# Spreading feed-forward parts over the half-steps of a unit of attention: a share for the half-step of the first product with V

## The chip, the cores and the metric

One of the eight cores of a Trainium2 chip runs the program. Times are device microseconds (us) of one execution, taken as the median of several runs; one further execution was recorded by the hardware profiler, and every row of a profile is from that one. The engines are TensorE (PE; its weight loads are PEld), VectorE (DVE), ScalarE (ACT), GpSimd (POOL) and SyncE (SP), which issues the DMAs.

## The reference

```python
x = A_x                                   # [1, 2048, 512]
mod = (silu(c) @ w_mod).reshape(1, 6, 1, 512)
sa, ca, ga, sb, cb, gb = mod's six rows
h = layernorm(x) * (1 + ca) + sa
q = (h @ wq) as 32 heads of 16            # k = h @ wk, v = h @ wv: one head of 16
p = softmax(q k^T / 4)                    # 2048 x 2048 for each head
x = x + ga * ((p @ v, heads side by side) @ wo)
h = layernorm(x) * (1 + cb) + sb
x = x + gb * ((sigmoid(h @ w_gate) * (h @ w_up)) @ w_down)     # F = 1792
```

Everything is float32. The kernel forms most products from numbers split into a high and a low half of 16 bits, in three passes (high x high, high x low, low x high).

## The kernel before

A first stage (`PLAN`, some 110 us) loads the input, makes k, V and the first queries, and begins the maxima. Then comes the main stage, which the change touches, and behind it a tail with what is left of the feed-forward layer for the last 512 rows.

**The main stage** runs over 32 units: 8 blocks of 256 queries by 4 groups of 8 heads. A unit has 16 steps of 128 keys, a step `s` has two half-steps `h`, so there are 1024 half-steps. In each of them the program emits for TensorE, in the order `ORDER = "a0", "s0", "c", "a1", "s1"`:

- `a0` and `a1`: scores whose maxima VectorE takes (`a_tile`, PSUM tiles `sa`, three banks, reduced into `mx`). They run more than a unit ahead.
- `s0` and `s1`: scores once more, transposed (`st_tile`, PSUM tiles `st`, two banks), of which ScalarE takes the exponential into `P`.
- `c`: the product of `P` with V (`pv`, PSUM tensor `craw`), two steps (`LAG`) behind the scores, in float32, followed by a hand-over: a matmul with a block of zeros (`nought`) on whose end the next product waits.
- a *piece*: so many *parts* of whatever else TensorE has to do (`piece`).

All of these are 64 x 32 tiles. The `a` and `s` of a half-step lie on one half of the rows, the product with V on the other, and in the next half-step the halves are exchanged. The order on TensorE, VectorE and ScalarE is that of the program (`keep`).

**A unit's end.** `craw` is one bank. After the last product of a unit (step `t = NKB - 1`, `h = 1`) ScalarE copies it out (`unit_end`, tile `cs`), and the first product of the next unit (`t = 0`, `h = 0`) waits for that copy. The exponentials behind it in ScalarE's queue come after it.

**Parts.** The other work comes in couples of two groups of matmuls that accumulate in two banks (`Couple`): one part is 8 matmuls of 64 x 32 tiles with 512 columns, four on either half of the rows. There are query couples (24 parts, tiles `pq`, before `FIRST = 140` steps are over), couples with wo (24, `po`), with gate and up (24, `pgu`) and with down (48 or 36, `pd`). `plan` takes the next couple when the one before is used up and asks `places` how many parts each half-step gets: the couple's two halves are laid out over as many half-steps as their weights times a rate come to (`RATE = 2.2` parts, `QRATE = 0.55` for query couples), and rounded cumulatively. `weight` gives the weight of one half-step. Before the change it is:

- 0 for the half-step of a unit's first product with V,
- `SWAP / RATE`, that is 5 parts, for that of the last product (1 for query couples),
- for the others what makes the sum of a unit 32 (1 for query couples, whose sum is 31).

`lead` carries what a couple is ahead or behind on to the next. For query couples the first three half-steps of a couple get nothing (`skip`).

Of the kernel before, what the change touches and what calls it, by code (L numbers as in the profile page):

```python
# [26 lines left out]
NKB = S // P  # L27
# [38 lines left out]
RATE = 2.2  # L66
# [2 lines left out]
AHEAD = 0, 0, 0, 0  # L69
MOST = 3  # L70
SWAP = 5
WSTEPS = 110
WLAST = 175
WLATE = 2
# [14 lines left out]
def adaln_mqa_glu_kernel(  # L89
# [928 lines left out]

    def weight(hb, q):
        s, h = divmod(hb, 2)
        t = (s - LAG) % NKB
        if s >= LAG and (t, h) == (0, 0):
            return 0.0
        if (t, h) == (NKB - 1, 1):
            return SWAP / RATE if not q else 1.0
        return 1.0 if q else (2 - SWAP / RATE + 2 * (NKB - 1)) / (2 * NKB - 2)

    def places(m, hb, rate, most, skip, part):  # L1030
        ws = []
        rate, most = rate / part, most / part
        while sum(ws) * rate < m + lead[0] / part - rate / 2 or sum(ws) * most < m:
            ws.append(0.0 if len(ws) < (skip or 0) else weight(hb + len(ws), skip is not None))
        lead[0] += part * (m - rate * sum(ws))
        ends = [round(m * sum(ws[:k + 1]) / sum(ws)) for k in range(len(ws))]
        return [k - z for z, k in zip([0] + ends, ends)]
# [28 lines left out]
    def plan(s, hb):  # L1066
        if run:
            return
        g = pick(s)
        if g is None:  # L1070
            lead[0] = 0.0
            return
        if g.stage == "tr":
            sizes = [4]
        else:
            q = g.stage == "q" and s < FIRST
            light = not q and g.stage == "gu" and s < 2 * NU * NKB + SKIP
            rate, most = (QRATE, 1) if q else (ERATE, 2) if light else (RATE, MOST)
            sizes = []
            for leg in range(2):  # L1080
                sizes += places(g.n // 2, hb + len(sizes), rate, most, (3 if leg == 0 else 0) if q else 0 if light else None, g.w)
            if hb + len(sizes) > 2 * len(units) * NKB:
                spare.insert(0, g)
                return
        at = 0
        for z in sizes:
            run.append((g, at, at + z))
            at += z
        assert at == g.n, (at, g.n, g.stage)
# [12 lines left out]
    for i, (b, o) in enumerate(units):  # L1102
# [11 lines left out]
        for kb in range(NKB):  # L1114
# [30 lines left out]
            while wdone < nw:  # L1145
                if wdone < nw - 4 and (wdone + 0.5) * WSTEPS > (s + 1) * (nw - 4):
                    break
# [68 lines left out]
```

## Time and profile before

| | |
|---|---|
| median of 3 runs | 1707.13 us (1706.41 to 1707.3) |
| the profiled execution's own time | 1703.12 us |
| its span, first to last instruction | 1701.3 us |
| busy: PE, PEld, DVE, ACT, POOL | 1657.1, 997.2, 1427.7, 1287.3, 610.2 us |
| mean granted TensorE clock | 0.993 |

A row of a group of instructions gives: line, engine, operation, output <- inputs, shapes, count | busy time in us, mean ns of one | idle time of the engine before them, with what ended it. A row of a timeline gives: start in us, length in us, engine, line, operation, names, count, and in brackets idle time ahead of it. A row of windows gives: the stretch, its length, then busy time and count of each engine, the granted clock, the DMA engines' busy share and GB/s. Most instructions go through one helper and so bear line 135; they are told apart by their tiles. Ends of matmuls are modelled, so the starts are the better measure.

### The profile page before, as it was taken

What the parts mean: (1) busy time and instruction counts of PE and PEld (TensorE: products, weight loads), DVE (VectorE), ACT (ScalarE), POOL (GpSimd) and SP (SyncE); (2) the same over time, 40 slices, a digit from 0 to 9 for tenths busy, and PEclk for the clock granted to TensorE, in tenths of its full rate; (3) what the DMA queues carried; (4) which work ended last, traced back from release to release, by engine and by line L of the source; (5) the groups of instructions that cost most, each with busy time, mean ns of one, the idle gap of its engine ahead of it and who ended that gap; (6) DMA issues with size and microseconds to landing.
All of it is one profiled execution on the core that took longest, in us unless ns stands there. A gap on an engine that the chain in (4) does not pass through costs nothing.

```text
span 1701.3 us, 88793 instructions
## 1 busy us (share of the span) xinstructions
PE 1657.1 (97%) x40226; PEld 997.2 (59%) x40226; DVE 1427.7 (84%) x2428; ACT 1287.3 (76%) x2335; POOL 610.2 (36%) x784
## 2 busy tenths in 40 slices
PE   6999999999999999999999999999999999999998
PEld 3335555555456666666656676666666676654443
DVE  7799999989999999999999999999999999912311
ACT  5558898878988888888888888888888888884100
POOL 4432554553242451232443232223442332132423
PEclk9989999999999999999999999999999999999999
DMA  7121333320121110111021110010121110011211
GB/s 243 54 62 49 107 104 99 110 77 21 29 62 50 58 54 14 40 28 28 28 77 52 50 42 13 28 37 25 38 77 41 52 53 16 23 47 52 87 50 38
DMA packets 86726, 94.12 MB, mean 55 GB/s; under 512 B 24916, under 2 KB 65868, under 8 KB 86348
## 3 DMA queue, kind: packets, MB, share of 16 engines
q1 hardware_dynamic: 86348, 88.44, 16.8%
q8 instruction: 315, 5.16, 1.3%
q14 instruction: 63, 0.52, 0.1%
HBM read 67.82 MB, written 16.24 MB: 49 GB/s over the span
## 4 chain that ended last, share of the span: by engine, by line
PE 81%; DVE 11%; ACT 3%; SPq 2%; DMA 2%; issue 1%; POOL 1%; POOLq 0%; ACTq 0%; DVEq 0%
PE craw L135 21%; PE pgu L135 15%; PE sa L135 13%; PE st L135 12%; DVE mx L135 8%; PE pd L135 7%; PE pgu L186 5%; PE pd L186 3%; PE po L135 2%; PE pq L135 2%; SPq L135 1%; ACT P L135 1%; DVE st L135 1%; DMA xall<-in_A_x_dram 1%; DMA lc<-lD 1%
## 5 line engine op out<-in xcount | busy, mean ns | idle before, releaser
L135 DVE TENSOR_REDUCE mx<-sa 128x1 f32<-128x512 f32 x2048 | 1288.6, 682 | 82.3 <-PE st L135 40.5
L135 ACT ACTIVATE P<-st 128x512 f32<-128x512 f32 x2048 | 1167.4, 597 | 226.2 <-PE st L135 168.6
L135 PE MATMUL craw<-P,V 64*32 64x512 f32 x8192 | 1094.7, 599 | 1.3 <-ACT cs L135 0.5
L135 PE MATMUL sa<-kp,qp 64*32 64x512 f16 (+1 forms) x7940 | 834.7, 379 | 13.1 <-DVE mx L135 12.4
L135 PE MATMUL st<-qp,kp 64*32 64x512 f16 x8192 | 837.6, 379 | 4.9 <-ACT P L135 4.2
L135 PEld LDWEIGHTS <-kp 64*32 64x32 f16 x8192 | 333.9, 91 | 215.9 <-issue 93.4
L135 PEld LDWEIGHTS <-qp 64*32 64x32 f16 (+1 forms) x7940 | 288.4, 92 | 149.6 <-issue 74.2
L135 PE MATMUL pgu<-h2h,gw 64*32 64x512 f16 x5248 | 285.4, 376 | 0.6
L135 PEld LDWEIGHTS <-gw 64*32 64x32 f16 x7872 | 181.7, 92 | 66.8 <-issue 25.1
L135 PEld LDWEIGHTS craw<-P,V 64*32 64x32 f32 x8192 | 184.0, 105 | 23.7 <-PE craw L135 4.1
L135 PE MATMUL pgu<-h2l,gw 64*32 64x512 f16 x2624 | 178.8, 376 | 1.2 <-issue 1.0
L135 PE MATMUL craw<-nought 64*32 64x1 f16 x1050 | 171.2, 163 | 0.0
L897 POOL TENSOR_SCALAR th<-th 128x512 f32<-128x512 f32 x41 | 25.4, 620 | 355.0 <-ACT th L135 298.2
L135 PEld LDWEIGHTS <-nought 64*32 64x32 f16 x1050 | 97.7, 93 | 71.9 <-issue 51.5
L556 POOL MEMSET qp<- 32x1024 f16 x60 | 56.7, 945 | 79.3 <-PE st L135 57.2
L320 POOL TENSOR_SCALAR wst<-wst 128x512 f32<-128x512 f32 x46 | 28.6, 621 | 155.5 <-DMA wst<-in_B_w_up_dram 103.2
L135 PE MATMUL pd<-wdl,gh 64*32 64x512 f16 x1152 | 79.2, 376 | 0.0
L135 PE MATMUL pd<-wdh,gh 64*32 64x512 f16 x1152 | 77.3, 376 | 0.1
L135 PE MATMUL pd<-wdh,gl 64*32 64x512 f16 x1152 | 76.6, 376 | 0.0
L186 PE MATMUL pgu<-h2h,gw 128*128 128x512 f16 x240 | 71.9, 379 | 1.5 <-DVE h2h L355 1.5
L891 ACT ACTIVATE th<-pgu 128x512 f32<-128x512 f32 x15 | 9.0, 597 | 82.1 <-PE pgu L186 82.1
L135 DVE COPY u<-pgu 128x512 f32<-128x512 f32 x41 | 28.0, 682 | 50.1 <-PE pgu L135 50.1
(160 smaller groups left out, 1436.9 us busy)
## 6 DMA issues: line engine op xcount, KB each, us to landing
gw<-wD SPq DMA_DIRECT2D x56, 512.0 KB
wD<-gw SPq DMA_DIRECT2D x14, 512.0 KB
wm<-in_w_mod_dram SPq DMA_DIRECT2D x6, 1024.0 KB
qp<-qD SPq DMA_DIRECT2D x192, 32.0 KB
qD<-q SPq DMA_DIRECT2D x16, 256.0 KB
xr<-in_A_x_dram SPq DMA_DIRECT2D x16, 256.0 KB
out_dram<-ot SPq DMA_DIRECT2D x16, 256.0 KB
raw<-cs SPq DMA_DIRECT2D x248, 16.0 KB
```

Source lines behind the costliest of these rows:

```text
L135: return (lambda *a, **k: keep(f_(*a, **k))) if pinned else f_
L186: pe.matmul(cut[0](self.bank) if cut else self.bank, l_, r_, start=(n == 0), stop=(n == self.n - 1))
L320: pool.tensor_scalar(w_, w_, SW, 0.0, op0=ALU.mult, op1=ALU.add)
L556: eng.memset(qp[j:j + 32], 0.0)
L891: act.activation(th, p_, AF.Tanh, scale=0.5 / (SH * SW))
L897: pool.tensor_scalar(th, th, 1.0, 1.0, op0=ALU.add, op1=ALU.mult)
```

## The change

Three things change in `weight` and what calls it: the half-step of a unit's first product with V gets the weight `FRESH = 0.9` instead of 0; the weight of the last half-step is 5 parts at whatever rate the couple has, so also for query couples; and the other half-steps' weight makes the sum of a unit 32 in both kinds. The rate is passed in, before it is divided by a group's width.

```diff
+FRESH = 0.9
...
-    def weight(hb, q):
+    def weight(hb, rate):
         s, h = divmod(hb, 2)
         t = (s - LAG) % NKB
         if s >= LAG and (t, h) == (0, 0):
-            return 0.0
+            return FRESH
         if (t, h) == (NKB - 1, 1):
-            return SWAP / RATE if not q else 1.0
-        return 1.0 if q else (2 - SWAP / RATE + 2 * (NKB - 1)) / (2 * NKB - 2)
+            return SWAP / rate
+        return (2 * NKB - FRESH - SWAP / rate) / (2 * NKB - 2)

     def places(m, hb, rate, most, skip, part):
-        ws = []
+        ws, full = [], rate
         rate, most = rate / part, most / part
         while sum(ws) * rate < m + lead[0] / part - rate / 2 or sum(ws) * most < m:
-            ws.append(0.0 if len(ws) < (skip or 0) else weight(hb + len(ws), skip is not None))
+            ws.append(0.0 if len(ws) < (skip or 0) else weight(hb + len(ws), full))
```

## The prediction

> **What bounds the kernel now.** I read the page first, then the windows of single units, then the timeline of unit boundaries.
>
> ```profile
> L135 DVE TENSOR_REDUCE mx<-sa 128x1 f32<-128x512 f32 x2048 | 1288.6, 682 | 82.3 <-PE st L135 40.5
> L135 ACT ACTIVATE P<-st 128x512 f32<-128x512 f32 x2048 | 1167.4, 597 | 226.2 <-PE st L135 168.6
> ```
>
> Both groups run 2048 times, twice in each of the 1024 half-steps of attention. Back to back a maximum costs VectorE 0.63 us (1288.6/2048) and an exponential costs ScalarE 0.57 us, so a half-step takes VectorE about 1.26 us whatever TensorE does. One more operation recurs, once per unit: the eviction cs of the bank that collects P times V.
>
> ```profile
> L135 ACT ACTIVATE cs<-craw x32: 590/597/603, 151.0 to 1559.3; 128x512 f32<-128x512 f32 x32
> ```
>
> From the first to the last of these lie 31 units: (1559.3 - 151.0)/31 = 45.4 us a unit. Two kinds of unit are to be told apart. The windows (length, then busy time and count of PE, PEld, DVE, ACT, POOL; granted clock) of one stretch with query couples and two units with feed-forward parts:
>
> ```profile
> 192.60:234.30 41.70, 40.36 (x934) 21.03 (x927) 39.82 (x70) 37.34 (x70) 19.51 (x26) 1.00 0.31 93
> ...
> 909.20:955.10 45.90, 45.90 (x1378) 30.85 (x1372) 43.20 (x72) 38.49 (x71) 14.73 (x17) 1.00 0.16 49
> 955.10:1001.00 45.90, 45.87 (x1380) 31.91 (x1366) 42.78 (x71) 38.55 (x71) 14.74 (x17) 1.00 0.16 49
> ```
>
> In the query unit VectorE is busy 39.82 of 41.70 us (95%): it sets the pace. In the feed-forward units it is busy 94%, and TensorE 100% by records whose ends are modelled. Which one paces can't be read off these shares; it is read off what one part more costs. Here are stretches of 28 half-steps (from the product with V of a unit's fourth half-step to that of its last), shortest load first; the count of matmuls grows by 8 for each part:
>
> ```profile
> 1335.53:1374.96 39.43, 39.40 (x1194) 1.00 0.18 55
> ...
> 1426.99:1466.49 39.50, 39.44 (x1205) 1.00 0.06 16
> ...
> 913.89:953.74 39.85, 39.85 (x1210) 1.00 0.18 55
> 1097.09:1137.14 40.05, 40.05 (x1214) 1.00 0.14 41
> 543.12:583.28 40.16, 40.15 (x1222) 1.00 0.21 61
> 1288.67:1329.23 40.56, 40.36 (x1222) 1.00 0.18 54
> ```
>
> 28 matmuls more (3.5 parts) go with (40.16 + 40.56)/2 - 39.43 = 0.93 us more: 0.27 us a part. So in the middle of a feed-forward unit TensorE paces at the margin, at the full clock (1.00). The price of a part by itself stands at the boundary at 955, where five parts run in a row:
>
> ```profile
> 954.62 0.75 PE L135 MATMUL pgu<-h2h,gw 64*32 64x512 f16 x16
> 955.05 0.54 PE L135 MATMUL pgu<-h2l,gw 64*32 64x512 f16 x8
> 955.06 0.59 ACT L135 ACTIVATE cs<-craw 128x512 f32<-128x512 f32 x1
> 955.26 0.75 PE L135 MATMUL pgu<-h2h,gw 64*32 64x512 f16 x16
> 955.69 0.45 PE L135 MATMUL sa<-kp,qp 64*32 64x512 f16 x4
> 955.85 0.60 PE L135 MATMUL craw<-P,V 64*32 64x512 f32 x4
> ...
> 956.13 0.45 PE L135 MATMUL sa<-kp,qp 64*32 64x512 f16 x4
> ...
> 956.34 0.45 PE L135 MATMUL st<-qp,kp 64*32 64x512 f16 x4
> ...
> 956.70 0.16 PE L135 MATMUL craw<-nought 64*32 64x1 f16 x1
> 956.71 0.40 PE L135 MATMUL sa<-kp,qp 64*32 64x512 f16 x4
> ...
> 957.11 0.40 PE L135 MATMUL st<-qp,kp 64*32 64x512 f16 x4
> 957.12 0.64 PE L135 MATMUL craw<-P,V 64*32 64x512 f32 x4
> 957.32 0.40 PE L135 MATMUL sa<-kp,qp 64*32 64x512 f16 x4
> ...
> 957.79 0.40 PE L135 MATMUL st<-qp,kp 64*32 64x512 f16 x4
> ```
>
> 40 matmuls from 954.62 to 955.69: 0.214 us a part. The five parts cover the eviction (955.06 to 955.65); the unit's first product with V starts at 955.85. After it come no parts, and TensorE runs ahead of ScalarE, which the eviction has put 0.6 us behind: the score matmuls of the next half-step that should follow 0.22 us after 956.71 start at 957.11, and the next at 957.79, 0.47 after the maximum's at 957.32 where 0.22 would do. In these holes, 0.18 and 0.25 us, and in the time that the first product has its rows to itself, TensorE has room that the middle of the unit lacks; the change puts parts there.
>
> **The change part by part.** No instruction is added or removed; parts move between half-steps. I went through the sequence of couples with the arithmetic of `places`, once with either `weight`. For feed-forward couples a middle half-step's share falls from 2.2 x 0.9909 = 2.18 parts to 2.2 x 0.9609 = 2.11, the first half-step's rises from 0 to 2.2 x 0.9 = 1.98, the last one's stays 5; a unit still gets 32 x 2.2. Rounded to whole parts, over units 9 to 31: first half-steps 0 to 42 (twice 1, twenty times 2), last ones 100 to 108, the middle 50 fewer. Half-steps of three parts fall from 120 to 74 in units 9 to 30. The same groups are left for the end, so nothing moves into the tail.
>
> (a) Middle: 50 x 0.21 = 10.5 us less. Ends: 0 if VectorE paced after all, 50 x 0.29 = 14.5 at somewhat over the slope above. I take the price of the part itself, since the stretches also differ in where couples begin.
>
> (b) Last half-step: 8 parts more, each at most 0.21 (1.7 us), at least 0 where the wait for cs covers it. I take half, 0.8.
>
> (c) First half-step. At 955: the first product leaves its rows with the hand-over at 956.70, and the next maximum's matmuls start at 956.71. Two parts ahead of them in TensorE's queue move these to 957.14, the score matmuls 0.22 later to 957.36 (ScalarE is no longer late by then) and the second product from 957.12 to 957.37: what follows it starts 0.25 late, and who waits for it is VectorE and ScalarE. Two more boundaries, at 1092 and at 584 (hand-over of the first half-step, product of the second, its hand-over):
>
> ```profile
> 1093.58 0.16 PE L135 MATMUL craw<-nought 64*32 64x1 f16 x1
> ...
> 1093.97 0.64 PE L135 MATMUL craw<-P,V 64*32 64x512 f32 x4
> ...
> 1094.88 0.16 PE L135 MATMUL craw<-nought 64*32 64x1 f16 x1
> 1095.13 0.41 PE L135 MATMUL pgu<-h2h,gw 64*32 64x512 f16 x8
> ```
>
> ```profile
> 586.00 0.16 PE L135 MATMUL craw<-nought 64*32 64x1 f16 x1
> ...
> 586.60 0.64 PE L135 MATMUL craw<-P,V 64*32 64x512 f32 x4
> ...
> 587.49 0.16 PE L135 MATMUL craw<-nought 64*32 64x1 f16 x1
> ```
>
> By the same count (0.67 us from the first hand-over to the second product) the product moves from 1093.97 to 1094.25 and its hand-over, 0.91 behind it, to 1095.16, where the next parts start at 1095.13 today: 0.03 late. At 584 it moves from 586.60 to 586.67: 0.07 late. The mean of 0.25, 0.03 and 0.07 is 0.12; times 22 boundaries 2.6 us. Ends: 0, and 42 x 0.21 = 8.8 if nothing is hidden.
>
> (d) Query couples (rate 0.55): the last half-step's weight goes from 1 to 5/0.55 = 9.1, so its parts go from 0 or 1 to 5, and other half-steps get 0.40 instead of 0.55. In units 0 to 4 and 6 the last half-step goes from 0,0,1,0,1,1 to 5,4,5,5,5,5 (unit 5 keeps 5). The boundary at 234, with one part:
>
> ```profile
> 233.10 0.64 PE L135 MATMUL craw<-P,V 64*32 64x512 f32 x4
> ...
> 233.98 0.45 PE L135 MATMUL pq<-h1h,wdh 64*32 64x512 f16 x8
> ...
> 234.94 0.63 PE L135 MATMUL craw<-P,V 64*32 64x512 f32 x4
> 234.97 0.40 PE L135 MATMUL sa<-kp,qp 64*32 64x512 f16 x4
> 235.39 0.61 PE L135 MATMUL craw<-P,V 64*32 64x512 f32 x4
> ```
>
> ```profile
> 236.13 3.16 DVE L135 TENSOR_REDUCE mx<-sa 128x1 f32<-128x512 f32 x5 [0.56 <-PE st L135]
> ```
>
> Five parts from 233.98 end at 235.05; two groups at 0.22 bring the product to 235.30 instead of 234.94: 0.36 late, and VectorE, which already sat idle 0.56 us until the product was done (235.39 + 0.61, and 0.13), sits idle that much longer. It paces here, so this isn't made up; with four parts it is 0.15. Sum 5 x 0.36 + 0.15 = 2.0 us. Fewer parts in the other query half-steps give nothing back, as VectorE hides them. Ends: 0 (the unit's spare 5% takes it up) and 6 x 5 x 0.21 = 6.3.
>
> Sum: -10.5 + 0.8 + 2.6 + 2.0 = -5.1 us. The profiled execution took 1703.12 us (span 1701.3 and 1.8 around it) and would take 1698.0; the median shown is 1707.13, 4.0 above it, and gives **1702.0**. The query couples end up to six steps earlier, and with them their evictions, their DMAs through SP and the first couple with wo; each of these waits for nothing that isn't long there, so I cost the shift at nothing.
>
> A rule against this: the Trainium skill, "TensorE: Matmul & The Clock Gate", section "The mechanism" of its part on packing small matmuls, has it that matmuls start and end strictly in program order. The rows at 956.13 and 956.70 differ from it in the starts: the hand-over stands ahead of those maximum matmuls in the program and starts 0.57 us after them. In the ends this trace agrees: VectorE begins with the maximum of 234.97 (ended 235.37) only at 236.13, after the product that stands ahead of it. Without overlap of the two row halves the sum would have 8.8 for (c); that is the second rival.
>
> **The rivals.**
> 1. *VectorE paces the middle of feed-forward units* (slower). Then (a) is worth 0, while its idle time at the boundaries grows by (b), (c) and (d): +5.4 us, 1712.5. It decides from where a part taken out saves less than 5.4/50 = 0.11 us. For it: 94% busy. Against: the six stretches, 0.27 a part.
> 2. *The first half-step hides nothing*: two parts push everything behind them by 0.43 us. -10.5 + 0.8 + 8.8 + 2.0 = +1.1, 1708.2. For it: the first half-step takes 1.27 us at 955 (955.85 to 957.12), near what VectorE needs for any half-step. Against: the holes ahead of 957.11 and 957.79.
> 3. *Three-part half-steps cost more than their matmuls* (slope near 0.29) *and query units absorb theirs*: -14.5 + 0.8 + 2.6 = -11.1, 1696.0. For it: the slope of the stretches. Against: VectorE's 95% in query units.
> 4. *The change doesn't do what it says*: shares lost in rounding. The counts speak against it; 1707.
>
> **How the numbers follow.** Forecast 0.45 (1699 to 1705), rival 1 0.15, rival 2 0.20, rival 3 0.15, rival 4 0.05. A measurement of this kernel can tell about 0.2% (3.4 us) from no change. Faster by more: 0.35 of the forecast's 0.45, and rival 3: 0.50. Within: 0.10 of the forecast, most of rival 2 and rival 4: 0.32. Slower: rival 1 and the rest: 0.18. The range takes in rival 3 and most of rival 1: 1696 to 1711.5.
>
> **What would show it.** (a) right: units around 909 and 955 last about 45.6 us, with fewer three-part half-steps; wrong: they keep 45.9. (c) right: parts stand between the first half-step's score matmuls and the next maximum's, and the second product starts about 1.55 us after the first (1.27 at 955 now); rival 2: the following half-steps lie 0.4 us later. (d) right: around 192 to 320 the last half-step takes 2.2 us instead of 1.84 (233.10 to 234.94), units 0.3 us longer; wrong: they keep about 41.7. Units of both kinds unchanged, or a wait for banks at a couple that begins in a first half-step, would make the forecast wrong.

## The result, and the profile after

| | before | after |
|---|---|---|
| median, with the first comparison's runs | 1706.84 us (4 runs) | 1697.35 us (4 runs, 1696.0 to 1698.17) |
| ratio, 95% interval | | 0.9944 [0.9926, 0.9961] |
| profiled execution, span | 1703.12, 1701.3 us | 1696.61, 1694.8 us |

The change makes the kernel 9.5 us faster; 5.1 were forecast. The groups that were read first before, now of the changed kernel (its helper has line 136):

```profile
L136 DVE TENSOR_REDUCE mx<-sa 128x1 f32<-128x512 f32 x2048 | 1282.8, 680 | 84.0 <-PE st L136 37.9
L136 ACT ACTIVATE P<-st 128x512 f32<-128x512 f32 x2048 | 1167.5, 597 | 215.7 <-PE st L136 150.2
```

The same work, with 10.5 us less idle time of ScalarE ahead of its exponentials (226.2 before). Where the time went is seen best when the span is cut at first products with V: that of unit 0, of unit 8 (where feed-forward parts begin) and of unit 31, and the last half-step's. Windows of TensorE alone (stretch, length, busy, matmuls, granted clock, DMA share, GB/s), first before, then after:

```profile
0.00:110.59 110.59, 91.32 (x623) 0.93 0.42 137
...
110.59:450.79 340.20, 330.77 (x7579) 0.99 0.24 73
450.79:1512.84 1062.05, 1054.36 (x30397) 1.00 0.14 41
1558.08:1701.30 143.22, 135.76 (x638) 0.99 0.17 55
```

```profile
0.00:115.03 115.03, 97.41 (x655) 0.87 0.40 132
...
115.03:450.74 335.71, 329.72 (x7546) 1.00 0.25 74
450.74:1504.89 1054.15, 1048.18 (x30399) 1.00 0.14 41
1550.01:1694.82 144.81, 137.35 (x638) 0.98 0.16 55
```

Units 8 to 30 are 7.9 us shorter and units 0 to 7 are 4.5 us shorter: 12.4 us in these two stages. The first stage is 4.4 us longer and the end 1.6, at a lower granted clock (0.87 against 0.93 in the first stage). Most of that varies from execution to execution, as the experiments below show, but not all: the first stage has 655 matmuls after the change and 623 before, which is four parts of 8 more. The weight of a last half-step applies to step 1 as well (`t = NKB - 1`), ahead of unit 0's first product with V, so five query parts stand there instead of one. From the main stage's first transposed scores to that product, before and after:

```profile
104.94 0.64 PE L135 MATMUL st<-qp,kp 64*32 64x512 f16 x4
...
109.81 1.01 PE L135 MATMUL pq<-h1h,wdh 64*32 64x512 f16 x8
...
110.59 1.09 PE L135 MATMUL craw<-P,V 64*32 64x512 f32 x4
```

```profile
108.00 0.65 PE L136 MATMUL st<-qp,kp 64*32 64x512 f16 x4
...
112.88 1.01 PE L136 MATMUL pq<-h1h,wdh 64*32 64x512 f16 x8
...
114.55 0.65 PE L136 MATMUL pq<-h1l,wdh 64*32 64x512 f16 x8
...
115.03 0.60 PE L136 MATMUL craw<-P,V 64*32 64x512 f32 x4
```

That is 7.03 us instead of 5.65, at a granted clock near 0.5. So 1.4 us of the longer first stage belong to the change, and of the 12.4 us some 11 remain.

**The start of a unit.** The boundary of unit 18, which began at 909.90 before, now with two parts in the first half-step (start, length, engine, then names and count):

```profile
906.20 0.60 PE L136 MATMUL craw<-P,V 64*32 64x512 f32 x4
...
906.70 0.45 PE L136 MATMUL st<-qp,kp 64*32 64x512 f16 x4
906.81 2.52 ACT L136 ACTIVATE P<-st 128x512 f32<-128x512 f32 x4 [0.53 <-PE st L136]
906.91 0.53 PE L136 MATMUL pgu<-h2h,gw 64*32 64x512 f16 x7
907.07 0.16 PE L136 MATMUL craw<-nought 64*32 64x1 f16 x1
907.10 0.59 PE L136 MATMUL pgu<-h2h,gw 64*32 64x512 f16 x9
...
907.48 0.62 PE L136 MATMUL craw<-P,V 64*32 64x512 f32 x2
907.49 0.38 PE L136 MATMUL sa<-kp,qp 64*32 64x512 f16 x1
...
907.71 0.41 PE L136 MATMUL st<-qp,kp 64*32 64x512 f16 x4
```

The two parts (16 matmuls from 906.91) stand where the forecast put them, but the second product starts at 907.48, 1.28 us after the first, not the 1.55 forecast. It starts together with the maximum's matmuls and ahead of the score matmuls (907.71), which stand before it in the program. Before, the score matmuls waited for ScalarE at that place of the next unit (957.11 in the prediction's lines), and the product, queued behind the wait, started 0.01 us after them. With the parts in front that wait is gone, and so is what it held up: over units 9 to 30 these score matmuls start 0.47 us after the maximum's in the mean before the change and 0.24 after it.

**The middle of a unit.** The same 28 half-steps of units 18 and 22 as before (39.85 us with 1210 matmuls, 40.05 with 1214):

```profile
910.44:949.73 39.29, 39.29 (x1194) 1.00 0.18 55
1092.56:1132.04 39.48, 39.46 (x1196) 1.00 0.14 41
```

16 and 18 matmuls fewer, 0.56 and 0.57 us less: 0.25 to 0.28 us a part of 8 matmuls in these two units; the sums over all units are further down.

**The end of a query unit.** Unit 2's last product, the five parts (40 matmuls; the first and the last group of them are shown) and the next unit's first product, which is unit 3's:

```profile
237.80 0.63 PE L136 MATMUL craw<-P,V 64*32 64x512 f32 x4
...
238.68 0.54 PE L136 MATMUL pq<-h1h,wdl 64*32 64x512 f16 x8
...
239.54 0.54 PE L136 MATMUL pq<-h1h,wdh 64*32 64x512 f16 x8
...
239.90 0.61 PE L136 MATMUL craw<-P,V 64*32 64x512 f32 x4
...
240.20 0.69 DVE L136 TENSOR_REDUCE mx<-sa 128x1 f32<-128x512 f32 x1 [0.48 <-PE sa L136]
```

2.10 us from product to product, as against 1.84 before: the five parts cost 0.26 us here. Yet units 0 to 7 became faster, and that is unit 6: 41.4 us instead of 47.0.

**The hole in unit 6.** Before the change, SyncE, GpSimd, VectorE and TensorE there:

```profile
361.48 6.25 SPq L135 DMA_DIRECT2D raw<-cs  x8
367.78 0.58 SPq L135 DMA_DIRECT2D wst<-in_B_w_down_dram  x1
```

```profile
371.08 0.62 POOL L320 TENSOR_SCALAR wst<-wst 128x512 f32<-128x512 f32 x1 [10.02 <-DMA wst<-in_B_w_down_dram]
...
374.48 0.62 POOL L320 TENSOR_SCALAR wst<-wst 128x512 f32<-128x512 f32 x1 [0.84 <-DMA wst<-in_B_w_down_dram]
...
378.24 2.51 POOL L832 TENSOR_TENSOR xr<-t,xr 128x512 f32<-128x512 f32 x2
```

```profile
379.56 0.69 DVE L135 BATCH_NORM_STATS2 st<-xr 128x6 f32<-128x512 f32 x1 [2.18 <-POOL xr L832]
```

```profile
381.10 0.40 PE L135 MATMUL sa<-kp,qp 64*32 64x512 f16 x4 [2.22 <-DVE mx L135]
```

The first couple with wo ended in unit 6, and its rows xr had to go through GpSimd. GpSimd stood 10 us on a weight load that SyncE issued only after the eight DMAs of a unit's end; xr came late, behind that split and the next (374.48); VectorE's statistics of xr, in order between maxima, stood 2.18 us; TensorE, out of banks for maxima, 2.22 us. And then, in this execution, it ran slowly, as the windows behind the hole show (the third is of the same kernel profiled once more, e9, right behind its hole):

```profile
381.00:384.00 3.00, 2.90 (x45) 0.56 0.00 0
384.00:387.00 3.00, 3.00 (x82) 0.87 0.00 0
...
386.42:389.83 3.41, 3.41 (x86) 1.00 0.00 0
```

The granted clock is 0.56 and 0.87 there: 3.4 us at 0.5. In e9 the hole was longer, 2.62 us, and the clock stayed at 1.00; unit 6 took 46.4 us there. Less their waits of VectorE (2.18 and 2.58) the two units last 44.85 and 43.84 us, so the slow clock cost about 1.0 us where it came. With the change that couple begins at step 90 instead of 96, its rows reach VectorE at the end of unit 5, and VectorE doesn't wait for them (GpSimd, then VectorE, after):

```profile
356.37 0.62 POOL L321 TENSOR_SCALAR wst<-wst 128x512 f32<-128x512 f32 x1 [5.48 <-DMA wst<-in_B_w_down_dram]
...
361.76 1.28 POOL L833 TENSOR_TENSOR xr<-t,xr 128x512 f32<-128x512 f32 x1
```

```profile
366.48 0.68 DVE L136 BATCH_NORM_STATS2 st<-xr 128x6 f32<-128x512 f32 x1
```

### The profile page after: what moved, and what is told of

Read it like the earlier page. It is cut to its first block, busy times and chain, and to the rows that moved or that the text cites. A ratio compares the mean times of both kernels' runs of the same rounds, so it can differ in the third digit from the quotient of the medians.

```text
span 1694.8 us, 88800 instructions
## 1 busy us (share of the span) xinstructions
PE 1657.4 (98%) x40227; PEld 1010.1 (60%) x40227; DVE 1422.2 (84%) x2428; ACT 1287.2 (76%) x2335; POOL 610.1 (36%) x784
## 4 chain that ended last, share of the span: by engine, by line
PE 85%; DVE 9%; ACT 2%; DMA 1%; issue 1%; SPq 1%; POOL 1%; POOLq 0%; ACTq 0%; DVEq 0%
PE craw L136 22%; PE pgu L136 16%; PE sa L136 14%; PE st L136 12%; PE pd L136 7%; DVE mx L136 7%; PE pgu L187 5%; PE pd L187 3%; PE po L136 3%; PE pq L136 2%; ACT P L136 1%; DMA xall<-in_A_x_dram 1%; DVE st L136 1%; SPq L136 1%; DVE h2h L136 0%
## 5 line engine op out<-in xcount | busy, mean ns | idle before, releaser
L136 PEld LDWEIGHTS <-kp 64*32 64x32 f16 x8192 | 337.5, 91 | 206.0 <-issue 78.3
L136 PE MATMUL pgu<-h2h,gw 64*32 64x512 f16 x5248 | 290.1, 376 | 0.9
```

Of the source, the lines that this page charges most:

```text
L136: return (lambda *a, **k: keep(f_(*a, **k))) if pinned else f_
```

## The experiments

From here the **theory** is: two separate gains, about 8 us of units 8 to 30 from the first half-step's share, about 4.5 of units 0 to 7 because the first couple with wo left the unit's end. Its rivals stand in the expectations. For each run the interval of the ratio is one to three us wide on either side. The lengths of the two stages are steadier, though each comes from one execution, and carry the verdicts on where time goes. They have two loose places: unit 0 varies by about 1 us (41.1 and 42.0 us in the two profiles of before) with how far a stretch at a granted clock of 0.5 (98.07 to 111.73 in the first of them) reaches into it, and units 25 and 26 together by up to 2 us. Below, "query stage" is from the first product with V of unit 0 to that of unit 8, "feed-forward stage" from there to that of unit 31.

| kernel | first stage | query stage | feed-forward stage | ratio to before, 95% interval |
|---|---|---|---|---|
| before | 110.6 | 340.2 | 1062.1 | |
| before, once more (e9) | 115.2 | 339.9 | 1061.8 | |
| the change | 115.0 | 335.7 | 1054.2 | 0.9944 [0.9926, 0.9961] |
| the change, once more (e10) | 118.0 | 335.6 | 1053.8 | 0.9927 [0.9913, 0.9941] |
| e1, feed-forward shares alone | 116.3 | 339.9 | 1053.9 | 0.9973 [0.9961, 0.9984] |
| e2, query shares alone | 113.9 | 336.6 | 1061.6 | 0.9992 [0.9984, 1.0001] |
| e3, query rate alone | 115.3 | 334.7 | 1062.9 | 0.9970 [0.9959, 0.9981] |
| e4, later split | 110.5 | 340.2 | 1061.5 | 0.9999 [0.9987, 1.0011] |
| e5, first half-step's weight 1.8 | 115.3 | 336.8 | 1056.0 | 0.9964 [0.9951, 0.9977] |
| e6, three parts in the last half-step | 114.3 | 336.5 | 1058.3 | 0.9970 [0.9957, 0.9983] |
| e7, loads a step earlier | 116.2 | 337.3 | 1059.2 | 0.9982 [0.9969, 0.9994] |
| e8, e1 and e3 together | 114.8 | 334.5 | 1055.1 | 0.9935 [0.9919, 0.9950] |
| e8 once more (e11) | 113.4 | 334.0 | 1053.4 | 0.9918 [0.9905, 0.9932] |
| e12, copy on VectorE | 114.5 | 342.6 | 1061.8 | 1.0011 [1.0000, 1.0022] |

**e1: the feed-forward couples' part alone.**

```diff
+        if rate == QRATE:
+            return 0.0 if s >= LAG and (t, h) == (0, 0) else 1.0
         if s >= LAG and (t, h) == (0, 0):
             return FRESH
```

> The feed-forward couples share as after the change (0.9 for the first half-step), the query couples as before it. Theory (two separate gains: about 8 us in units 8 to 30 from the first half-step, about 4.5 us in units 0 to 7 because the first couple with wo no longer lies across a unit's end): from the first product of unit 8 to that of unit 31 1054 us as after the change (1062 before), from the first product of unit 0 to that of unit 8 340 us as before it, the wait of VectorE for xr in unit 6 is still there; about 8 us faster than before. Rival A (all of the gain is the first half-step, the query couples cost the 2 us forecast): faster than the changed kernel by 2 us, 11 us below before. Rival B (the gain is the query couples'): within 1 us of before.

The window of the feed-forward stage:

```profile
456.14:1510.02 1053.88, 1048.05 (x30399) 1.00 0.14 41
```

1053.9 as with the change, and the query stage 339.9 as before it. VectorE's wait for xr is still there, 1.66 us. The theory holds for the stages; rival B falls, and of rival A, that this kernel would beat the changed one, the opposite is seen. But the whole kernel got faster by less than the 8 us expected: the interval of the ratio allows 2.7 to 6.7 us, and no run says where the rest went.

**e2: the query couples' part alone.**

```diff
-            return FRESH
+            return FRESH if rate == QRATE else 0.0
...
-        return (2 * NKB - FRESH - SWAP / rate) / (2 * NKB - 2)
+        return (2 * NKB - (FRESH if rate == QRATE else 0.0) - SWAP / rate) / (2 * NKB - 2)
```

> The query couples share as after the change (5 parts in the last half-step), the feed-forward couples as before it. Theory: units 0 to 7 take 335.7 us instead of 340.2, units 8 to 30 stay at 1062; about 4.5 us faster than before. Rival A (the forecast's term for the query couples): 2 us slower than before, units 0 to 4 longer by 0.36 each and nothing gained in unit 6. Rival B: 9 us faster.

```profile
113.87:450.47 336.60, 330.30 (x7546) 1.00 0.24 73
```

336.6, between the theory's 335.7 and no change, on the theory's side; the feed-forward stage stays. Units 1 to 4 take 167.3 us as against 165.7 (165.1 in e9): a cost is there, 1.6 to 2.2 us in four units (0.5 to 1.9 in the two profiles of the change). Units 5 to 7 take 127.8 as against 133.4 (132.8): more than that comes back. Ahead of unit 0, though, the five parts cost 1.7 us here (7.36 us where before has 5.65), so of the 3.6 us some 1.9 remain. That agrees with the medians (1706.21 to 1704.35), whose interval reaches from 2.7 us faster to 0.2 slower: rival A falls, and so does the 4.5 us faster that was expected of the whole kernel.

**e3: the couple moved without the five parts.**

```diff
-QRATE = 0.55
+QRATE = 0.6
```

> The kernel before with one number changed: query couples at 0.60 parts a half-step instead of 0.55, so that the first couple with wo begins at step 89 instead of 96, away from the end of unit 5, while no last half-step gets five parts. Theory: the hole in unit 6 goes as with the change, and the 0.3 us that each unit of the changed kernel pays for five parts isn't paid: units 0 to 7 take 333 to 335 us, 5 to 6 us faster than before. Rival (it is the five parts in the last half-steps that help units 0 to 7): no faster than before, 340 us.

```profile
115.27:450.00 334.73, 328.70 (x7577) 1.00 0.25 74
```

334.7 us, with last half-steps of 1.81 us in the mean of units 0 to 4 and 6 as before (2.02 with the change). Ahead of unit 0 it takes 5.65 us, as before. So it isn't the five parts that help the query stage; they cost, and beginning the couples earlier gains. (The rate moves all query couples, not only the one with wo.)

**e4 and e7: the load that GpSimd waits for.** First (e4) the split was put off by two steps, then (e7) the load was issued about a step earlier:

```diff
-WLATE = 2
+WLATE = 4
```

```diff
-                if wdone < nw - 4 and (wdone + 0.5) * WSTEPS > (s + 1) * (nw - 4):
+                if wdone < nw - 4 and (wdone + 0.1) * WSTEPS > (s + 1) * (nw - 4):
```

> The kernel before with one number changed: GpSimd splits a weight four steps after its load is issued, instead of two. Nothing of the couples moves. Theory (in unit 6 GpSimd stands 10 us on a load of w_down that SyncE issues late, behind the eight loads of a unit's end; xr is added behind it, and VectorE and TensorE wait 2.2 us for that): the waits of 10 us and 2.2 us go, units 0 to 7 take 336 to 338 us, 2 to 4 us faster than before, units 8 to 30 stay at 1062. Rival (the hole belongs to the place of the couple with wo at the unit's end, whatever GpSimd waits for): units 0 to 7 stay at 340.

> The kernel before with one number changed: every weight load of the main stage is issued about one step earlier, so that the load of w_down at step 98 stands ahead of the ten DMAs of unit 5's end on SyncE instead of behind them. The couples stay where they are. (Splitting later left GpSimd's order as it was, so this is the second try.) Theory (GpSimd's 10 us on that load makes the hole in unit 6): the waits of 10 us on GpSimd and of 2.2 us on VectorE and TensorE go, and with them the granted clock of 0.56 behind them; unit 6 takes 43 to 44 us instead of 47, units 0 to 7 336 to 337 us instead of 340.2, units 8 to 30 stay at 1062. Rival (the hole belongs to the couple's place at the unit's end): unit 6 stays at 47.

e4 told nothing of the cause: GpSimd's order, which isn't the program's, came out the same, the wait was 10.7 us and VectorE's 2.4 us. In e7 GpSimd, then VectorE:

```profile
378.28 0.62 POOL L320 TENSOR_SCALAR wst<-wst 128x512 f32<-128x512 f32 x1 [10.56 <-DMA wst<-in_B_w_down_dram]
...
382.04 1.28 POOL L832 TENSOR_TENSOR xr<-t,xr 128x512 f32<-128x512 f32 x1
```

```profile
383.49 0.68 DVE L135 BATCH_NORM_STATS2 st<-xr 128x6 f32<-128x512 f32 x1
```

The wait on GpSimd didn't go, against the expectation: it moved to the next load. But only one split stood between it and xr, not two, and VectorE no longer waited: it takes up xr 17.0 us after unit 6's first product with V, instead of 19.2. Unit 6 took 43.6 us instead of 47.0 (46.4 in e9) with the couple in its old place, so the rival that unit 6 stays at 47 falls. The 3.4 us are about the wait of 2.2 and the slow clock behind it. What is left to the 41.4 of the change, some 2.2 us, goes with the couple's place, and these runs don't say how. One candidate, which no run isolates, is that TensorE stands 1.07 us for ScalarE at the couple's first matmuls in before and in e7 alike, and doesn't in the change. The feed-forward stage of e7 is 2.9 us shorter too, 2.1 of it in units 25 and 26, where no weight load is left. That is the spread of these units: in the two profiles of one kernel, e8 and e11, unit 25 differs by 1.9 us.

**e5 and e6: the sizes.** Two numbers of the changed kernel, one at a time:

```diff
-FRESH = 0.9
+FRESH = 1.8
```

```diff
-SWAP = 5
+SWAP = 3
```

> The changed kernel with the first half-step's weight doubled, 1.8 instead of 0.9: 92 parts instead of 42 in the first half-steps of units 9 to 31, 40 fewer in the middle ones, 10 fewer in the last ones. Theory (the room at a unit's start holds about two parts, and a part beyond pushes all that follows by 0.21 us): first two half-steps of units 9 to 30 longer by 8 to 11 us, the middle shorter by about 8 and the last by 2, units 8 to 30 within 2 us of the changed kernel's 1054. Rival (the first half-step still hides what is put there): another 8 us shorter, 1046.

> The changed kernel with three parts instead of five for the last half-step: 62 parts instead of 108 there in units 9 to 30, 46 more in the middle. Theory (a part in the middle costs its 0.21 us, and the last half-step can't be shorter than the wait for the copied bank allows, 1.84): middle 9.7 us longer, last half-steps 2 to 3 us shorter, units 8 to 30 about 7 us longer than with the change (1061), units 0 to 7 shorter by 1 to 2 us since three query parts fit into that wait. Rival (VectorE paces the middle): middle unchanged, 1051.

Sums over units 9 to 30 of the times from one product with V to the next, and of the parts that fall between them:

| | parts: first two, middle, last | us: first two half-steps | us: middle (29) | us: last |
|---|---|---|---|---|
| before | 47, 1329, 100 | 60.9 | 917.6 | 41.6 |
| the change | 85, 1283, 108 | 61.3 | 907.6 | 43.3 |
| e5 | 130, 1254, 98 | 70.5 | 902.1 | 41.7 |
| e6 | 88, 1326, 62 | 60.9 | 914.4 | 40.9 |

In the change 38 more parts in the first two half-steps cost 0.3 us; in e5 another 45 cost 9.2, 0.2 a part. The room holds about two parts a unit, as the theory has it. The middle gave back 10.0 us for 46 parts (0.22), in e5 another 5.5 for 29 (0.19), and in e6 it took 6.8 for 43 (0.16). These prices can't be told apart: units 25 and 26, which vary between executions, make 2.2 of the 10.0 us, and without them the prices are 0.18, 0.24 and 0.16. TensorE paces the middle at about 0.2 us a part. e6's feed-forward stage is 4.1 us longer than the change's where 7 was expected, on the theory's side; e5's 1.8 longer. Both rivals fall. One thing expected of e6 is missed: three query parts do fit into the wait (last half-steps of 1.81 us again), yet the query stage is 0.8 us longer than the change's, not shorter; units 5 to 7 take 129.1 us there as against 128.0. It saves 0.5 us ahead of unit 0 (6.51 us against 7.03).

**e8 and e11: the two gains without the five parts.** e1's edit, and with it:

```diff
-QRATE = 0.55
+QRATE = 0.6
```

> The feed-forward couples of the change together with query couples that share as before it, at 0.60 parts a half-step (the two edits that gained alone). Theory (the two gains are separate, and five query parts in a last half-step cost 0.2 to 0.4 us a unit): units 0 to 7 334.7 us, units 8 to 30 1054; 1 us less than the changed kernel in the main stage, some 13 us less than before. Rival (one takes the other's room): units 8 to 30 above 1056 or units 0 to 7 above 336.

> The changed kernel once more, on one chip with the next. Theory as before: units 0 to 7 335.7 us, units 8 to 30 1054; 9 to 12 us faster than before.

> The feed-forward share of the change with query couples at 0.60 and shared as before it, once more, beside the changed kernel on one chip. Theory: units 0 to 7 1 us shorter than the changed kernel's, the rest the same: 0 to 3 us faster than it. Rival: no difference that these runs can tell, or slower.

e10 repeats the change: 335.6 and 1053.8 us in the two stages, and 11.6 us faster than before by the medians. In e8 and e11 the query stage is 1.2 to 1.6 us shorter than the changed kernel's, the feed-forward stage the same within 1 us, and ahead of unit 0 they don't pay the 1.4 to 1.7 us. On one chip e11 took 1692.86 us (1692.19 to 1693.23) and the changed kernel 1694.43 (1692.7 to 1697.36); the ranges overlap and so do the intervals of the ratios. It has the lowest median of the kernels here, but that it beats the change is not shown. The gains add: 8.2 (e1) and 5.5 (e3) make 13.7, and e8 and e11 are 12.7 and 14.8 below before in the two stages.

**e9: the first stage.**

> The kernel before, profiled once more. Theory (the stage ahead of the first product with V has the same instructions in the same order in all these kernels, and its length varies with the granted clock from execution to execution): that stage takes anything from 110 to 116 us, units 0 to 7 340 us and units 8 to 30 1060 to 1063 as in the first profile. Rival (that stage is 4 us longer because of the change): again 110.6.

115.2 us where the first profile had 110.6, with the other stages as before. Over the nine profiles that have one query part ahead of unit 0, and so the same matmuls in this stage, it lies between 110.5 and 116.3, at granted clocks of 0.93 down to 0.87: it varies by almost 6 us with the execution. But the expectation is wrong that all these kernels have the same instructions there. In these nine the stretch from the first transposed scores to unit 0's first product is 5.65 us every time; in the change, e10, e2 and e5, with five parts, it is 7.03 to 7.36, and in e6, with three, 6.51. So the first stage does say something of the change, and only a stretch of it that is the same in every execution shows it. Against this profile the changed kernel's span is 10.5 us shorter (1705.3 to 1694.8).

**e12: whose lag makes the room.**

```diff
-        raw_c["out"] = act.activation(cs, raw_c["c"], AF.Identity)
+        raw_c["out"] = dve.tensor_copy(cs, raw_c["c"])
```

> The kernel before with the copy of the bank at a unit's end made by VectorE instead of ScalarE. Theory (the room in the first half-step is there because the copy puts ScalarE 0.6 us behind): the score matmuls of the next half-step no longer wait for it, and the first half-steps of units 9 to 30, 30.1 us in sum, get shorter by 2 to 4 us; VectorE, idle there about 0.5 us, takes most of the copy's 0.68 without delay. Rival (the first half-step is as long as VectorE needs for any half-step, about 1.26): its sum stays at 30 or grows by up to 22 x 0.68 = 15 us.

In units 9 to 30 the first half-steps come down from 30.1 to 28.3 us, just short of what the theory expected, and the rival's growth is not seen; the second ones grow by 1.1, the last ones by 2.1, the middle falls by 2.7, and the query stage, which VectorE paces, is 2.4 us longer. Moving the copy gains nothing. Nor does it take ScalarE's lag away. Behind the hand-over of the first half-step of unit 18:

```profile
917.04 2.52 ACT L135 ACTIVATE P<-st 128x512 f32<-128x512 f32 x4 [0.61 <-PE st L135]
...
917.34 0.39 PE L135 MATMUL sa<-kp,qp 64*32 64x512 f16 x4
...
917.68 0.40 PE L135 MATMUL st<-qp,kp 64*32 64x512 f16 x4
```

The score matmuls still start 0.34 us after the maximum's, where 0.22 would do; in the mean over units 9 to 30 it is 0.38, as against 0.47 before and 0.24 with the change. ScalarE begins late here without the copy, having stood 0.61 us until its scores came. So the copy makes less than half of the wait that the two parts fill; that the five parts ahead of the first scores make the rest is likely, and not shown.

## Why the prediction was right, and where it was not

- *TensorE paces the middle of feed-forward units*: right, at about the price that was taken. -10.0 us measured in the middle against -10.5 for (a), but 2.2 of the 10.0 lie in units 25 and 26, which vary by nearly as much between executions; that the two figures meet so closely is partly luck.
- *(b), parts in last half-steps*: +1.7 us against +0.8; the upper end.
- *(c), the first half-step*: mis-sized. +0.3 us against +2.6 (first half-steps +1.9, second ones -1.6). The step that failed is "0.67 us from the first hand-over to the second product": it let the product start after the score matmuls, as the second product of a unit did in the old trace. It did so there only because the score matmuls waited for ScalarE. Without the wait the product starts ahead of them, on the other half of the rows (907.48 and 907.71). The old trace shows that as well, one product earlier: at 955.85, 0.06 us ahead of the score matmuls behind which it stands in the program (955.91).
- *(d), the query couples*: that five parts in a last half-step cost something was right. They cost 0.26 us at the boundary of 239.90 against 0.36, and 1.3 us in sum over the last half-steps of units 0 to 4 and 6 against 2.0. The working doesn't add up: five parts to 235.05 and two groups at 0.22 give 235.49, not 235.30. It has the same flaw as (c): the product starts at 239.90, ahead of the score matmuls (239.98), and waits for neither group whole. And (d) left out one last half-step, that of step 1, ahead of unit 0: another 1.4 us in the change, 1.7 in e10.
- *The shift*: what failed is the sentence beside (d), that the couples' inputs are long there, "so I cost the shift at nothing". The first couple with wo had made VectorE wait 2.2 us for xr, and the shift was worth 5.4 us in units 5 to 7. e7, where the couple stays and VectorE doesn't wait, gives 3.2 us of that; the cause of the rest stays open. The long half-steps of unit 6 stood in the trace of before, and the waits on xr in its list of waits.
- The forecast's -5.1 became -9.5 by the medians (-11.6 in e10). By the two profiles it is -7.9 in units 8 to 30, -5.4 in units 5 to 7, +0.9 in units 0 to 4 and +1.4 ahead of unit 0: -11.0. The direction and the main term (a) were foreseen; nearly half of the gain came from a term that was put at nothing. That the median of 1697.35 lies in the range from 1696 is partly luck: the range reached down there only for rival 3, whose reason fell, and in e10 the same kernel took 1694.43.
- *Rival 1* (VectorE paces the middle) fell with the 10.0 us of the middle, and in e5 and e6. *Rival 2* (nothing hidden) fell in the change itself and would have been right for the parts of e5. *Rival 3* named about the right size for the wrong reason: a part in the middle cost about 0.2 us, not 0.29, and the query units did pay.
- The rule of the Trainium skill that was weighed (matmuls start and end in program order, "TensorE: Matmul & The Clock Gate", "The mechanism") differs from these rows in the starts once more, and the forecast, which argued against it, kept to its order in one place by starting the product after the score matmuls.

## What to carry to other kernels

A step that is moved is moved past other queues too: before costing it at nothing, look in the trace at what its consumers wait for where it stands, since a wait of 2 us that ends by the move, with what hangs on it, can be worth more than the edit costs. Where one engine lags behind after a unit's boundary, the room on another is limited and is filled by a few parts; twice as many cost their full price. And when two profiles differ in a stage that seems untouched, count its instructions before calling it so (623 and 655 matmuls here), look for a stretch of it that repeats exactly, and run the old kernel once more.

## What the runs showed of the hardware that was not expected

- Holes on TensorE of 1.68, 2.22 and 2.44 us (e12, before, e4) were each followed by 3.4 us at a granted clock of 0.5; holes of 1.63 and 2.62 us at the same place (e1, e9) were not, and the clock stayed at 1.00. So the length of the hole alone didn't decide it.
- The first stage with the same matmuls took 110.5 to 116.3 us in nine profiles. The feed-forward stage, at a granted clock of 1.00, repeats within 0.4 us in the two profiles of before and in those of the change, and within 1.7 us in those of e8 and e11, where it is one unit that differs.
- Matmuls on the two halves of the rows can start in another order than the program's: 907.48 ahead of 907.71 here, 955.85 ahead of 955.91 and 956.13 ahead of 956.70 in the kernel before.
